# A fused attention and two-mixture kernel: the first unit gets its own stage order, its loads go to two queues, and the order of the first weight loads changes

## The chip, the cores and the metric

The kernel runs on one core of a Trainium2 chip. The metric is the time of one execution in device microseconds (us), and the time of a kernel is the median of three runs. A core has a matrix engine (TensorE, PE in the rows, with its weight loads as PEld), a vector engine (VectorE, DVE), an activation engine (ScalarE, ACT), GpSimd (POOL) and a queue engine (SyncE, SP) that mostly starts loads and stores. ScalarE can start loads too. Each engine works through its own list of instructions in order, and semaphores tie the lists together.

## The reference, cut to what matters

```python
# attention: B, H, S, D = 2, 8, 768, 48
for t in range(S):
    state = alpha[:, :, t, :, None] * state + np.einsum('bhd,bhe->bhde', k[:, :, t], v[:, :, t])
    y[:, :, t] = np.einsum('bhd,bhde->bhe', q[:, :, t], state)
# first mixture: 1536 tokens, 384 features, 4 experts, 1024 hidden
p = domain_probs / (domain_probs.sum(-1, keepdims=True) + 1e-09)
for e in range(E):
    out += p[:, e:e + 1] * (np.maximum(x @ w1[e], 0.0) @ w2[e])
# second mixture: 8 experts, the best two of each token by noisy logits, the same two products
```

## The kernel before, in words

The attention is done in chunks of 128 tokens. Tokens come in seven units of 128 or 256 tokens (`sizes`). A unit is worked through in groups of 128 x 256 values: unit 0 has two groups, here called 0 and 1, unit 1 has the four groups 2 to 5. A group goes through seven stages: `decays` (transpose alpha, running products on VectorE), `keys` (transpose k, scale it on VectorE to K, then on ScalarE to G), `queries` (transpose q, scale to Q), `scores` (G times Q, masked on VectorE to M), `keys_back` (transpose K back, copied by ScalarE to Kn), `states` (Kn times v, added by VectorE to the running state S) and `outputs` (Q times S plus M times v, copied by ScalarE to xn). When all groups of a unit are done, `back` transposes xn into xh and xl, which feed the dense products. `plan()` gives every stage of every group a step number, and `stream()` issues the stages step by step. The first two groups are "near": their stages lie closer together than those of later groups.

While the first attention units are worked through, TensorE also runs `busy(n)`: n filler products of ones by ones whose result nobody reads. `IDLE` says ahead of which stage how many stand.

The first mixture's expert 0 starts as soon as unit 0 is back. Its first phase of 128 tokens is eight dense products f0 to f7 (`hidden`, line 475, straight from the loaded weights `raw`), with the stages of groups 2 to 5 set between them by `drive()`, and then its second products (`product`, lines 494 to 496). Each dense product's result is copied by ScalarE (hh) and VectorE (hl). At each step of `drive()`, `W.step` may prepare one part of the weights: ScalarE casts it to the high part (line 142) and GpSimd subtracts for the low part (line 143). Expert 0's parts 0 to 3 are the four quarters of w2, loaded into spare room of the tile `acc`; parts 4 to 7 are the quarters of w1, loaded into `raw`. They are prepared in the order 0 to 7. The loads of unit 0, of unit 1 and of these eight parts are issued on SP in the order of one loop near the end of the function, which is the only thing that sets their order.

Of the kernel before, what the change touches and what calls it, by code (L numbers as in the profile page):

```python
# [10 lines left out]
F32 = mybir.dt.float32  # L11
# [6 lines left out]
OP = mybir.AluOpType  # L18
AX = mybir.AxisListType

P = 128
# [7 lines left out]
def kernel(  # L29
# [28 lines left out]
    BM = UM // P  # L58
    KD = DM // P
    KF = FF // P  # L60
    HP = H // 2
# [5 lines left out]
    const = ctx.enter_context(tc.tile_pool(name="const", bufs=1))  # L67
# [5 lines left out]
    def ps(tag, bufs=1):  # L73
        return psum.tile([P, 512], F32, tag=tag, name=tag, bufs=bufs)
# [111 lines left out]
    def busy(n):  # L186

        t = ps("g", 4)
        for _ in range(n):
            nc.tensor.matmul(t.rearrange("x (c i) -> x c i", c=4), ones_b, ones_b[:, None, :].to_broadcast([P, 4, P]),  # L190
                             start=True, stop=True)

    busy(14)
    ident = const.tile([P, P], F32, name="ident")
    make_identity(nc, ident)
    tri = const.tile([P, P], F32, name="tri")
# [16 lines left out]
    apool = att.enter_context(tc.tile_pool(name="apool", bufs=1))  # L213
# [4 lines left out]
    for nm, n in (("a", 2), ("k", 1), ("q", 1)):  # L218
        for i in range(n):
            t = apool.tile([P, BM, H, 64], F32, name=f"x_{nm}{i}", tag=f"x_{nm}{i}")  # L220
# [8 lines left out]
    V = {}  # L229

    def inputs(nm, u):
        if nm == "a":
            return X[nm, u % 2]
        return X[nm, 0] if u else early[:, "kq".index(nm)]

    def load_unit(u, names, p0=0, p1=HP):

        if u >= NU:
            return
        b, h0 = divmod(starts[u], S)  # L240
        hs = slice(2 * p0, 2 * p1)
        for nm in names:
            if nm == "v":
                V[u] = apool.tile([P, BM, H, D], F32, tag="v", name="v", bufs=2)
            for c in range(sizes[u] // P):
                frm = src[nm][b, hs, h0 + c * P:h0 + (c + 1) * P, :].rearrange("h p d -> p h d")
                if nm == "v":
                    nc.sync.dma_start(V[u][:, c, hs], frm)
                    continue
                nc.sync.dma_start(inputs(nm, u)[:, c, hs, :D], frm)  # L250


    prob = const.tile([P, NB, E1], F32, name="prob")
    nc.scalar.dma_start(prob, moe_domain_probs.rearrange("(b p) e -> p b e", p=P))
    noise = const.tile([P, NB, E2], F32, name="noise")
    nc.scalar.dma_start(noise, moe2_noise.rearrange("(b p) e -> p b e", p=P))
    wgn = const.tile([P, KD, 2 * E2], F32, name="wgn")
    nc.scalar.dma_start(wgn[:, :, :E2], moe2_w_gate.rearrange("(c p) e -> p c e", p=P))
    nc.scalar.dma_start(wgn[:, :, E2:], moe2_w_noise.rearrange("(c p) e -> p c e", p=P))

    W = Weights()

# [2 lines left out]
    for i in range(2):  # L265
        t = apool.tile([P, UM], F32, name=f"suffix{i}")
# [11 lines left out]
    def attention(u):  # L278

        b, h0 = divmod(starts[u], S)  # L280
# [10 lines left out]
            return slice(i * P, (i + 1) * P)  # L291

        def transposed(nm, g):
            t = ps("tr", 2)
            for i, (p, c) in enumerate(groups[g]):
                nc.tensor.transpose(t[:, at(i)], inputs(nm, u)[:, c, 2 * p:2 * p + 2, :].rearrange("x h d -> x (h d)"), ident)  # L296
            return t[:, :UM]
# [43 lines left out]

        def scores(g):
            A, K, Q, G, rc = st[g]
            t = [ps("sc0"), ps("sc1")]
            for i in range(BM):
                for j in range(2):
                    rows = slice(64 * j, 64 * j + D)
                    nc.tensor.matmul(t[j][:, at(i)], G[rows, at(i)], Q[rows, at(i)], start=True, stop=True)  # L348
            for j in range(2):
                M = apool.tile([P, BM, P], F32, tag=f"M{j}", name="M")  # L350
                nc.vector.tensor_mul(M, t[j][:, :UM].rearrange("x (c i) -> x c i", c=BM),
                                     tri[:, None, :].to_broadcast([P, BM, P]))
                st[g, j] = M
# [23 lines left out]

        def outputs(g):
            A, K, Q, G, rc = st[g]
            t = ps("sc1")  # L380
            for i, (p, c) in enumerate(groups[g]):
                inter = not (first and c == 0)
                if inter:
                    nc.tensor.matmul(t[:, i * 2 * D:(i + 1) * 2 * D], Q[:, at(i)], St[p][:, slot(c), :],  # L384
                                     start=True, stop=False)
                for j in range(2):
                    o = i * 2 * D + j * D
                    nc.tensor.matmul(t[:, o:o + D], st[g, j][:, i, :], V[u][:, c, 2 * p + j, :], start=not inter,  # L388
                                     stop=not inter or j == 1)
            if g == 0:  # L390
                st["xn"] = apool.tile([P, BM, DM], F32, tag="xn", name="xn")
            xn = st["xn"]
            p = groups[g][0][0]
            n = 2 * D * BM // UB
            nc.scalar.activation(xn[:, :UB, 2 * p * D:2 * p * D + n],
                                 t[:, :UB * n].rearrange("x (c d) -> x c d", c=UB), AF.Copy)
# [34 lines left out]
    suffixes = itertools.cycle(suffix)  # L431

    rows_at = {}
    NEAR = 2

    IDLE = {(2, 0): 5, (1, 0): 5, (2, 1): 2, (1, 1): 4, (2, 2): 4, (1, 2): 2, (0, 0): 1, (0, 1): 1, (0, 2): 1}

    def plan():
        at = {}
        base = 0  # L440
        k = 0
        for u in range(NU):
            n, UB, stages, back = attention(u)
            for g in range(n):
                near = k < NEAR
                for order, (stage, off) in enumerate(zip(stages, (5, 4, 1, 3, 3, 2, 0) if near else (7, 6, 1, 5, 3, 2, 0))):
                    at.setdefault(base + off, []).append((order, k, stage, g))
                end = base + (5 if near else 7)
                base += 2 if near else 3
                k += 1  # L450
            for c in range(UB):
                at.setdefault(end + 1 + c, []).append((-1, k, back, c))
            rows_at[u] = end + 1 + UB
        return at

    steps = plan()

    def stream():
        for i in range(max(steps) + 1):
            for order, k, f, g in sorted(steps.get(i, ()), key=lambda z: z[:2]):  # L460
                busy(IDLE.get((order, k), 0))
                f(g)
            yield

# [65 lines left out]
    def drive(main, side=None, n_main=1, n_side=1, bg=None, finish=True):  # L530


        due = 0.0
        pace = n_main / n_side if n_side else float("inf")
        wait = pace
        for _ in main:
            if bg is not None:
                bg()
            due += 1
            while side is not None and due >= wait:  # L540
                due -= wait
                try:
                    said = next(side)
                    wait = pace if said is None else said
                except StopIteration:
                    side = None
        if side is not None and finish:
            for _ in side:
                pass


    psm = const.tile([P, NB], F32, name="psm")
    nc.vector.reduce_sum(psm, prob, axis=AX.X)
    nc.vector.tensor_scalar(psm, psm, 1e-9, None, op0=OP.add)
    nc.vector.reciprocal(psm, psm)
    nc.vector.tensor_mul(prob, prob, psm[:, :, None].to_broadcast([P, NB, E1]))

    for i in range(2):
        load_unit(0, "akq", i * HP // 2, (i + 1) * HP // 2)
    load_unit(0, "v")  # L560
    for what in ("a", "k", "q", 4, 0, 5, "v", 1, 6, 2, 7, 3):
        if type(what) is int:
            W.fetch(what)
        else:
            load_unit(1, what)
    W.n_raw = 2 * NG
# [3 lines left out]
    def until(i):  # L570
        nonlocal now
        while now < i:
            now += 1
            next(rows_now, None)
            yield

    for _ in until(rows_at[0]):
        if now >= 15 and W.n_prep < 4:
            W.prep()

    def n_moe(n):
        return KF + n // P * (KF // 2)
# [4 lines left out]
    for i, (t0, n) in enumerate(phases):  # L587
        for _ in until(rows_at[unit_of(t0 + n)]):
            pass
        nxt = rows_at[unit_of(sum(phases[i + 1]))] if i + 1 < len(phases) else now  # L590
        drive(moe1(0, t0, n), until(nxt), n_moe(n), (nxt - now) * 1.1, W.step)
    att.close()

    hst = ExitStack()
    hidden_in.append((hst.enter_context(tc.tile_pool(name="hpool", bufs=1, side="right")), 4 * P))


    NS = E2 * SB
    BL = 3
# [554 lines left out]
```

## Time and profile before

| | |
|---|---|
| median of three runs | 764.56 us (764.32 to 765.46) |
| the profiled execution | 764.46 us, its span 762.7 us |
| TensorE busy | 98% of the span |
| VectorE, ScalarE, GpSimd busy | 46%, 32%, 21% |

The span is the time from the first to the last instruction; 1.8 us of the execution lie around it. Busy shares are averages over the whole span: TensorE is the engine to look at, and only the first 40 us have other engines in its way.

### The profile page before, as it was taken

The page shows a single profiled execution, that of the slowest core. Times are in us where ns is not written, and L with a number is a line of the kernel's source. Part 1 is how long each engine was busy: PE and PEld are TensorE (multiplying, and loading weights), DVE is VectorE, ACT ScalarE, POOL GpSimd, SP SyncE. Part 2 cuts the span into 40 slices and gives each one's busy share as a digit, 9 for nine tenths or more (in the row PEclk, how much of TensorE's full clock was granted, in tenths as well). Part 3 has the DMA queues.
Part 4 walks back from the last instruction along what each step waited for, and adds up shares of the span by engine and source line. Part 5 has one row for each costly group of instructions (what it writes and reads, how often), then busy time and mean ns, then how long its engine had stood idle before and what let it go on. Part 6 is the DMA issues. An engine that isn't in the chain of part 4 may idle for free.

```text
span 762.7 us, 11958 instructions
## 1 busy us (share of the span) xinstructions
PE 750.6 (98%) x4658; PEld 707.6 (93%) x4658; DVE 351.4 (46%) x864; ACT 246.0 (32%) x481; POOL 160.6 (21%) x174
## 2 busy tenths in 40 slices
PE   9999999999999999999999999999999999999996
PEld 5899999999998989899899999989999999999996
DVE  5877566663222131222212346366745554654641
ACT  2643322232311031211223323333525444444430
POOL 2520000001510023100124100011352424424331
PEclk9999999999999999999999999999999999999999
DMA  9836212100620012100023300011763554654710
GB/s 187 221 75 125 52 32 43 22 1 8 209 75 1 0 42 83 43 0 1 22 63 103 94 21 12 32 42 29 220 206 122 186 161 148 212 161 136 228 63 32
DMA packets 97998, 66.97 MB, mean 88 GB/s; under 512 B 57577, under 2 KB 94500, under 8 KB 97936
## 3 DMA queue, kind: packets, MB, share of 16 engines
q1 hardware_dynamic: 89008, 51.92, 24.6%
q0 software_dynamic: 5024, 14.13, 5.8%
q8 instruction: 39, 0.64, 0.4%
q10 hardware_dynamic: 3904, 0.10, 0.4%
q14 instruction: 23, 0.19, 0.1%
HBM read 56.69 MB, written 9.82 MB: 87 GB/s over the span
## 4 chain that ended last, share of the span: by engine, by line
PE 93%; DVE 5%; ACT 1%; issue 0%; POOL 0%; POOLq 0%; DVEq 0%
PE g L480 13%; PE g L479 13%; PE g L481 13%; PE g L494 10%; PE g L496 10%; PE g L495 10%; PE g L994 3%; PE g L996 3%; PE g L995 3%; PE sc L388 2%; PE tr L296 2%; PE sc L348 2%; PE tr L927 1%; PE sc L362 1%; PE sc L384 1%; PE g L190 1%
## 5 line engine op out<-in xcount | busy, mean ns | idle before, releaser
L485 ACT ACTIVATE hh<-g 128x384 fp32r<-128x384 f32 (+8 forms) x200 | 96.9, 485 | 281.2 <-PE g L481 261.6
L486 DVE SCALAR_TENSOR_TENSOR hl<-g,hh 128x384 fp32r<-128x384 f32 (+8 forms) x200 | 109.5, 550 | 159.5 <-ACT hh L485 154.1
L494 PE MATMUL g<-w2h,hl 128*128 128x384 f32 x464 | 161.7, 348 | 0.0
L496 PE MATMUL g<-w2h,hh 128*128 128x384 f32 x464 | 156.5, 337 | 0.0
L495 PE MATMUL g<-w2l,hh 128*128 128x384 f32 x464 | 156.4, 337 | 0.0
L479 PE MATMUL g<-xh,w1l 128*128 128x512 f32 (+2 forms) x360 | 127.0, 353 | 0.0
L480 PE MATMUL g<-xl,w1h 128*128 128x512 f32 (+2 forms) x360 | 124.4, 346 | 0.0
L481 PE MATMUL g<-xh,w1h 128*128 128x512 f32 (+2 forms) x360 | 124.3, 345 | 0.0
L143 POOL TENSOR_TENSOR w1l<-raw,w1h 128x768 fp32r<-128x768 f32 x16 | 29.3, 1841 | 280.2 <-ACT w1h L142 280.2
L494 PEld LDWEIGHTS g<-w2h,hl 128*128 128x128 f32 x464 | 87.3, 188 | 0.5
L495 PEld LDWEIGHTS g<-w2l,hh 128*128 128x128 f32 x464 | 87.4, 188 | 0.3
L496 PEld LDWEIGHTS g<-w2h,hh 128*128 128x128 f32 x464 | 87.2, 188 | 0.0
L523 DVE SCALAR_TENSOR_TENSOR acc<-g,prob,acc 128x384 f32<-128x384 f32 x36 | 22.2, 618 | 119.7 <-PE g L496 119.7
L480 PEld LDWEIGHTS g<-xl,w1h 128*128 128x128 f32 x360 | 67.8, 188 | 6.3 <-DVE xl L413 0.3
L481 PEld LDWEIGHTS g<-xh,w1h 128*128 128x128 f32 x360 | 67.7, 188 | 6.3
L479 PEld LDWEIGHTS g<-xh,w1l 128*128 128x128 f32 x360 | 67.8, 188 | 6.0
L479 PE MATMUL g<-xth,w1l 128*128 128x256 f32 (+6 forms) x216 | 73.2, 339 | 0.0
L480 PE MATMUL g<-xtl,w1h 128*128 128x256 f32 (+6 forms) x216 | 71.4, 331 | 0.1
L481 PE MATMUL g<-xth,w1h 128*128 128x256 f32 (+6 forms) x216 | 71.3, 330 | 0.0
L142 ACT ACTIVATE w2h<-raw 128x768 fp32r<-128x768 f32 x44 | 36.4, 843 | 35.3 <-issue 23.0
L945 POOL DMA_INDIRECT out_dram<-yo,si_c x26 | 26.1, 1004 | 87.1 <-DVE yo L944 80.9
L994 PE MATMUL g<-hh,w2l 128*128 128x432 f32 (+4 forms) x120 | 43.3, 361 | 0.0
(193 smaller groups left out, 1056.1 us busy)
## 6 DMA issues: line engine op xcount, KB each, us to landing
raw<-in_moe_w_dram SPq DMA_DIRECT2D x92, 384.0 KB, 4.3
v<-in_v_dram SPq DMA_DIRECT2D x12, 192.0 KB, 2.9
out_dram<-zero SPq DMA_DIRECT2D x1, 2304.0 KB
x2d<-acc SPq DMA_DIRECT2D x12, 192.0 KB, 4.5
x_a<-in_alpha_dram SPq DMA_DIRECT2D x20, 96.0 KB, 2.1
x_k<-in_k_dram SPq DMA_DIRECT2D x18, 96.0 KB, 2.6
x_q<-in_q_dram SPq DMA_DIRECT2D x18, 96.0 KB, 2.7
acc<-in_moe_w_dram SPq DMA_DIRECT2D x4, 384.0 KB, 7.1
```

Source lines behind the costliest of these rows:

```text
L142: nc.scalar.activation(hi, r, AF.Copy)
L143: (nc.gpsimd if e < E1 or own else nc.vector).tensor_sub(lo, r, hi.bitcast(F32))
L479: nc.tensor.matmul(t[:, :n], wl, hx[:, kd, t0:t0 + n], start=(kd == 0), stop=False)
L480: nc.tensor.matmul(t[:, :n], wh, lx[:, kd, t0:t0 + n], start=False, stop=False)
L481: nc.tensor.matmul(t[:, :n], wh, hx[:, kd, t0:t0 + n], start=False, stop=(kd == KD - 1))
L485: nc.scalar.activation(hh[:, :n], t[:, :n], AF.Relu)
L486: nc.vector.scalar_tensor_tensor(hl[:, :n], t[:, :n], 0.0, hh.bitcast(F32)[:, :n], op0=OP.max, op1=OP.subtract)
L494: nc.tensor.matmul(t[:m, :DM], hl[:, o:o + m], wh, start=(f == 0), stop=False)
L495: nc.tensor.matmul(t[:m, :DM], hh[:, o:o + m], wl, start=False, stop=False)
L496: nc.tensor.matmul(t[:m, :DM], hh[:, o:o + m], wh, start=False, stop=(f == KF - 1))
L945: nc.gpsimd.indirect_dma_start(out=parts_of_out[s], out_offset=bass.IndirectOffsetOnAxis(ap=SLOT[e * SB + s][2][:n, e * SB + s:e * SB + s ...
L994: nc.tensor.matmul(t[:, :n], wl, hh[:, :n], start=(f == 0), stop=False)
```

## The change

Unit 0's groups get step numbers of their own (`NEAR`), in which the transposed-back keys and the states come last, behind `back`. Their k and q loads are issued by ScalarE instead of SP. 21 of the 39 fillers go. The loads of the noise and of the gate weights move from the front to behind the last phase of expert 0, the sum of the probabilities moves behind expert 0's first eight dense products, and the probabilities are loaded by SP. Some tiles of unit 0 are taken from the four banks of the dense products ("g") and no longer from "tr", "sc0" and "sc1". And the loop that loads unit 1 and the eight weight parts has another order.

```diff
-    busy(14)
+    busy(9)
...
-    def load_unit(u, names, p0=0, p1=HP):
+    def load_unit(u, names, p0=0, p1=HP, queue=nc.sync):
...
+    for i in range(2):
+        load_unit(0, "a", i * HP // 2, (i + 1) * HP // 2)
+        load_unit(0, "kq", i * HP // 2, (i + 1) * HP // 2, nc.scalar)
+    load_unit(0, "v")
 
     prob = const.tile([P, NB, E1], F32, name="prob")
-    nc.scalar.dma_start(prob, moe_domain_probs.rearrange("(b p) e -> p b e", p=P))
     noise = const.tile([P, NB, E2], F32, name="noise")
-    nc.scalar.dma_start(noise, moe2_noise.rearrange("(b p) e -> p b e", p=P))
...
-            t = ps("tr", 2)
+            t = ps("g", 4) if u == 0 and (nm, g) in (("q", 0), ("a", 1)) else ps("tr", 2)
...
-            t = [ps("sc0"), ps("sc1")]
+            t = [ps("g", 4), ps("g", 4)] if u == 0 and g else [ps("sc0"), ps("sc1")]
...
-    NEAR = 2
-
-    IDLE = {(2, 0): 5, (1, 0): 5, (2, 1): 2, (1, 1): 4, (2, 2): 4, (1, 2): 2, (0, 0): 1, (0, 1): 1, (0, 2): 1}
+    NEAR = ({"decays": 0, "keys": 0, "queries": 0, "scores": 2, "outputs": 4, "keys_back": 7, "states": 8},
+            {"decays": 0, "keys": 1, "queries": 1, "scores": 3, "outputs": 5, "keys_back": 8, "states": 9})
+    FAR = {"decays": 0, "keys": 1, "queries": 2, "keys_back": 3, "scores": 5, "states": 6, "outputs": 7}
...
+    IDLE = {("scores", 0): 2, ("scores", 1): 5, ("back", 1): 2}
...
-    psm = const.tile([P, NB], F32, name="psm")
-    nc.vector.reduce_sum(psm, prob, axis=AX.X)
...
-    for what in ("a", "k", "q", 4, 0, 5, "v", 1, 6, 2, 7, 3):
+    for what in ("a", "k", 4, "q", 5, "p", "v", 6, 7, 0, 1, 2, 3):
...
-        drive(moe1(0, t0, n), until(nxt), n_moe(n), (nxt - now) * 1.1, W.step)
+        drive(moe1(0, t0, n, None if i else probabilities), until(nxt), n_moe(n), (nxt - now) * 1.1, W.step)
...
+    nc.sync.dma_start(noise, moe2_noise.rearrange("(b p) e -> p b e", p=P))
+    nc.sync.dma_start(wgn[:, :, :E2], moe2_w_gate.rearrange("(c p) e -> p c e", p=P))
```

On ScalarE, from the back-transposed unit 0 on, the list of before reads as follows (x32 is the 128 x 384 piece of `acc`; `w2h<-acc` is the cast of a w2 part, `hh<-g` the copy behind a dense product, `G<-K` and `Kn<-tr` belong to the attention's groups):

```order
L411 ACTIVATE acc<-g 128x384 [waits PE_49]
L412 ACTIVATE xh<-g 128x3x128
L321 ACTIVATE G<-K,rc 128x128 [waits DVE_49]
L321 ACTIVATE G<-K,rc 128x128
L485 ACTIVATE hh<-g 128x128 [waits PE_49]
L142 ACTIVATE w2h<-acc 128x768 [waits DMAHW2_49]
L485 ACTIVATE hh<-g 128x128 [waits PE_49]
L142 ACTIVATE w2h<-acc 128x768 [waits DMAHW6_49]
L339 ACTIVATE Kn<-tr 128x256 [waits PE_49,Activation_49]
L485 ACTIVATE hh<-g 128x128 [waits PE_49]
L142 ACTIVATE w2h<-acc 128x768 [waits DMAHW0_49]
```

And in the changed kernel, from the same place on:

```order
L412 ACTIVATE acc<-g 128x384 [waits PE_49]
L413 ACTIVATE xh<-g 128x3x128
L498 ACTIVATE hh<-g 128x128 [waits PE_49]
L142 ACTIVATE w2h<-acc 128x768 [waits DMAHW4_49]
L340 ACTIVATE Kn<-tr 128x256 [waits PE_49]
L498 ACTIVATE hh<-g 128x128 [waits PE_49]
L142 ACTIVATE w2h<-acc 128x768 [waits DMAHW5_49]
L322 ACTIVATE G<-K,rc 128x128 [waits DVE_49,Activation_49]
L322 ACTIVATE G<-K,rc 128x128
L340 ACTIVATE Kn<-tr 128x256 [waits PE_49]
L498 ACTIVATE hh<-g 128x128 [waits PE_49]
L142 ACTIVATE w2h<-acc 128x768 [waits DMAHW6_49]
```

The casts of the w2 parts stand at the same dense products as before, but the Kn of unit 0's two groups, which stood far ahead of the first cast, now stand behind the first and the second one.

On SP, behind the loads of unit 0 and the first four of unit 1, the list of before reads (a `raw` load is a w1 part, an `acc` load from `in_moe_w_dram` a w2 part):

```order
L250 DMA x_q_114<-in_q_dram 128x8x48 [waits DMAHW0_49]
L119 DMA raw<-in_moe_w_dram 128x3x256 [waits DMAHW1_49]
L124 DMA acc<-in_moe_w_dram 128x2x384 [waits DMAHW2_49]
L119 DMA raw<-in_moe_w_dram 128x3x256 [waits DMAHW3_49]
L248 DMA v<-in_v_dram 128x8x48 [waits DMAHW4_49]
L248 DMA v<-in_v_dram 128x8x48 [waits DMAHW5_49]
L124 DMA acc<-in_moe_w_dram 128x2x384 [waits DMAHW6_49]
L119 DMA raw<-in_moe_w_dram 128x3x256 [waits DMAHW7_49]
L124 DMA acc<-in_moe_w_dram 128x2x384 [waits DMAHW0_49]
```

And now:

```order
L250 DMA x_q_109<-in_q_dram 128x8x48 [waits DMAHW5_49]
L119 DMA raw<-in_moe_w_dram 128x3x256 [waits DMAHW6_49]
L569 DMA prob<-in_moe_domain_probs_dram 128x12x4 [waits DMAHW7_49]
L248 DMA v<-in_v_dram 128x8x48 [waits DMAHW0_49]
L248 DMA v<-in_v_dram 128x8x48 [waits DMAHW1_49]
L119 DMA raw<-in_moe_w_dram 128x3x256 [waits DMAHW2_49]
L119 DMA raw<-in_moe_w_dram 128x3x256 [waits DMAHW3_49]
L124 DMA acc<-in_moe_w_dram 128x2x384 [waits DMAHW4_49]
L124 DMA acc<-in_moe_w_dram 128x2x384 [waits DMAHW5_49]
```

The first w2 part was the second weight load on the queue; it is now the fifth, behind all four w1 parts and all of unit 1.

On TensorE, behind the first two dense products (the first `g<-acc,raw` here ends f1), the changed kernel has this (`sc<-v,Kn` is `states`, `sc<-Q,G` is `scores`, `tr<-ident,K` is `keys_back`):

```order
L488 MATMUL g<-acc,raw 128x128 x3
L363 MATMUL sc_346<-v,Kn 128x96 [waits Activation_49]
L363 MATMUL sc_346<-v,Kn 128x96
L297 MATMUL tr<-ident,x_k_107 128x128 [waits PE_49]
L297 MATMUL tr<-ident,x_k_107 128x128
L338 MATMUL tr<-ident,K 128x128 [waits DVE_49]
L338 MATMUL tr<-ident,K 128x128
L488 MATMUL g<-acc,raw 128x128 [waits DMAHW6_49]
L488 MATMUL g<-acc,raw 128x128 x2
L363 MATMUL sc_379<-v,Kn 128x96 [waits DVE_49,Activation_49]
L363 MATMUL sc_379<-v,Kn 128x96
L349 MATMUL sc_387<-Q,G 128x128 [waits DVE_49,PE_49]
```

In the kernel before, the `states` of groups 0 and 1 stood ahead of the first dense product, with fillers around them; no filler stands in this stretch now. From the `states` of group 5 on, TensorE's list is the same in both kernels to the end.

## Rows read from the trace of the kernel before

**Rows 1.** Busy time by stretch: busy us per engine (instructions), then clock, DMA share, GB/s.

```profile
0.00:10.00 10.00, 8.53 (x39) 4.11 (x39) 4.75 (x18) 1.98 (x3) 4.07 (x20) 1.00 0.95 124
10.00:20.00 10.00, 9.66 (x70) 6.91 (x68) 6.99 (x25) 3.26 (x10) 0.00 (x0) 1.00 1.05 251
20.00:30.00 10.00, 9.25 (x78) 7.99 (x79) 7.76 (x27) 6.46 (x17) 6.22 (x4) 1.00 0.88 249
40.00:200.00 160.00, 159.43 (x1229) 152.86 (x1228) 93.92 (x277) 49.44 (x127) 12.57 (x7) 1.00 0.24 52
```

**Rows 2.** Timeline, 0 to 28.5 us: first fillers, first scan, first dense product, three casts.

```profile
1.13 4.90 PE L190 MATMUL g<-ones_b 128*128 128x512 bf16 x14 [1.13 <-DVE ones_b L185]
...
4.51 1.01 PEld L190 LDWEIGHTS <-ones_b 128*128 128x128 bf16 x5 [0.28 <-issue]
...
6.36 0.73 DVE L312 TENSOR_TENSOR_SCAN suffix<-tr,tri 128x127 f32<-128x127 f32 x2 [1.00 <-PE tr L296]
...
20.23 0.94 PE L475 MATMUL g<-acc,raw 128*128 128x128 f32 x6 [0.34 <-ACT acc L411]
...
22.61 0.83 ACT L142 ACTIVATE w2h<-acc 128x768 fp32r<-128x768 f32 x1
...
26.23 0.84 ACT L142 ACTIVATE w2h<-acc 128x768 fp32r<-128x768 f32 x1 [0.71 <-DMA acc<-in_moe_w_dram]
```

**Rows 3.** Timeline of TensorE, 27 to 41 us, between the last waits and the merge.

```profile
27.53 0.72 PE L348 MATMUL sc<-Q,G 48*128 48x128 f32 x8
...
29.00 0.69 PE L362 MATMUL sc<-v,Kn 128*128 128x96 f32 x4 [0.39 <-DVE M L351]
...
30.62 0.36 PE L384 MATMUL sc<-S,Q 128*128 128x96 f32 x2
...
31.90 0.40 PE L296 MATMUL tr<-ident,x_k 128*128 128x128 f32 x2
...
32.14 0.83 PE L475 MATMUL g<-acc,raw 128*128 128x128 f32 x6
...
32.90 0.71 PE L348 MATMUL sc<-Q,G 48*128 48x128 f32 x8
...
40.04 0.58 PE L362 MATMUL sc<-v,Kn 128*128 128x96 f32 x4
```

**Rows 4.** DMA queues in the first 8 us: packets, MB, share of 16 engines.

```profile
q10 hardware_dynamic: 3904, 0.10, 34.4%
```

**Rows 5.** Instruction groups by shape, 5.6 to 40.1 us, ScalarE, then VectorE.

```profile
L321 ACT ACTIVATE G<-K,rc 128x128 f32<-128x128 f32 x14 | 4.9, 394 | 8.5 <-DVE K L319 8.4
L142 ACT ACTIVATE w2h<-acc 128x768 fp32r<-128x768 f32 x4 | 3.4, 840 | 0.7 <-DMA acc<-in_moe_w_dram 0.7
L339 ACT ACTIVATE Kn<-tr 128x256 f32<-128x256 f32 x6 | 2.3, 376 | 1.6 <-PE tr L337 1.5
...
L312 DVE TENSOR_TENSOR_SCAN suffix<-tr,tri 128x127 f32<-128x127 f32 x14 | 5.1, 407 | 1.8 <-PE tr L296 1.5
L314 DVE TENSOR_TENSOR_SCAN A<-tr,tri 128x128 f32<-128x128 f32 x14 | 5.0, 398 | 0.0
L351 DVE TENSOR_TENSOR M<-sc,tri 128x256 f32<-128x256 f32 x12 | 4.5, 416 | 0.1
L319 DVE TENSOR_TENSOR K<-tr,suffix 128x256 f32<-128x256 f32 x7 | 2.9, 410 | 0.0
L372 DVE COPY S<-sc 48x48 f32<-48x48 f32 x8 | 1.6, 205 | 2.3 <-PE sc L362 1.2 <-PE tr L296 1.1
```

**Rows 6.** Timeline of VectorE, 5 us: the last of the four probability instructions.

```profile
5.14 0.21 DVE L556 TENSOR_TENSOR prob<-prob,psm 128x48 f32<-128x48 f32 x1
```

**Rows 7.** The gate weights' readers: first and last start in us.

```profile
L652 PEld LDWEIGHTS sc<-wgn,x2T x72: 187/192/192, 419.9 to 520.3; 128*128 128x128 f32 x72
```

**Rows 8.** Busy time at the end of the span, columns as in Rows 1.

```profile
756.00:758.00 2.00, 0.70 (x5) 0.39 (x3) 0.62 (x1) 0.00 (x0) 0.36 (x1) 1.00 0.03 6
759.00:760.00 1.00, 0.00 (x0) 0.00 (x0) 0.00 (x0) 0.00 (x0) 0.00 (x0) 0.50 0.37 129
```

More of the change, by code (lines that the diff above doesn't have):

```diff
@@ L247, in load_unit @@
                 if nm == "v":
-                    nc.sync.dma_start(V[u][:, c, hs], frm)
+                    queue.dma_start(V[u][:, c, hs], frm)
                     continue
-                nc.sync.dma_start(inputs(nm, u)[:, c, hs, :D], frm)
+                queue.dma_start(inputs(nm, u)[:, c, hs, :D], frm)
+    for i in range(2):
+        load_unit(0, "a", i * HP // 2, (i + 1) * HP // 2)
+        load_unit(0, "kq", i * HP // 2, (i + 1) * HP // 2, nc.scalar)
+    load_unit(0, "v")
     prob = const.tile([P, NB, E1], F32, name="prob")
-    nc.scalar.dma_start(prob, moe_domain_probs.rearrange("(b p) e -> p b e", p=P))
     noise = const.tile([P, NB, E2], F32, name="noise")
-    nc.scalar.dma_start(noise, moe2_noise.rearrange("(b p) e -> p b e", p=P))
     wgn = const.tile([P, KD, 2 * E2], F32, name="wgn")
-    nc.scalar.dma_start(wgn[:, :, :E2], moe2_w_gate.rearrange("(c p) e -> p c e", p=P))
-    nc.scalar.dma_start(wgn[:, :, E2:], moe2_w_noise.rearrange("(c p) e -> p c e", p=P))
     W = Weights()
@@ L349, in scores @@
             for j in range(2):
-                M = apool.tile([P, BM, P], F32, tag=f"M{j}", name="M")
+                M = apool.tile([P, BM, P], F32, tag=f"M{j}", name="M", bufs=2)
                 nc.vector.tensor_mul(M, t[j][:, :UM].rearrange("x (c i) -> x c i", c=BM),
@@ L379, in outputs @@
             A, K, Q, G, rc = st[g]
-            t = ps("sc1")
+            t = ps("g", 4) if u == 0 and g else ps("sc1")
             for i, (p, c) in enumerate(groups[g]):
@@ L433 @@
     rows_at = {}
-    NEAR = 2
-    IDLE = {(2, 0): 5, (1, 0): 5, (2, 1): 2, (1, 1): 4, (2, 2): 4, (1, 2): 2, (0, 0): 1, (0, 1): 1, (0, 2): 1}
+    NEAR = ({"decays": 0, "keys": 0, "queries": 0, "scores": 2, "outputs": 4, "keys_back": 7, "states": 8},
+            {"decays": 0, "keys": 1, "queries": 1, "scores": 3, "outputs": 5, "keys_back": 8, "states": 9})
+    FAR = {"decays": 0, "keys": 1, "queries": 2, "keys_back": 3, "scores": 5, "states": 6, "outputs": 7}
+    ORDER = ("outputs", "states", "keys", "scores", "keys_back", "queries", "decays")
+    IDLE = {("scores", 0): 2, ("scores", 1): 5, ("back", 1): 2}
     def plan():
         at = {}
-        base = 0
+        base = 4
         k = 0
@@ L444, in plan @@
             for g in range(n):
[L445 to L449, printed above, removed]
+                offs = NEAR[k] if k < len(NEAR) else {nm: base + off for nm, off in FAR.items()}
+                if k == len(NEAR):
+                    offs["keys_back"] = 9
+                for order, (stage, nm) in enumerate(zip(stages, ORDER)):
+                    if k == 0 and nm in ("keys", "queries"):
+                        order += 10
+                    elif k == 1 and nm == "decays":
+                        order += 20
+                    elif k == 0 and nm == "decays":
+                        order = 0
+                    at.setdefault(offs[nm], []).append((order, k, stage, g, nm))
+                end = offs["outputs"]
+                if k >= len(NEAR):
+                    base += 3
                 k += 1
             for c in range(UB):
-                at.setdefault(end + 1 + c, []).append((-1, k, back, c))
+                at.setdefault(end + 1 + c, []).append((-1, k - 1, back, c, "back"))
             rows_at[u] = end + 1 + UB
@@ L459, in stream @@
         for i in range(max(steps) + 1):
-            for order, k, f, g in sorted(steps.get(i, ()), key=lambda z: z[:2]):
-                busy(IDLE.get((order, k), 0))
+            for order, k, f, g, nm in sorted(steps.get(i, ()), key=lambda z: z[:2]):
+                busy(IDLE.get((nm, k), 0))
                 f(g)
@@ L549, in drive @@
                 pass
-    psm = const.tile([P, NB], F32, name="psm")
-    nc.vector.reduce_sum(psm, prob, axis=AX.X)
[L554 to L560, printed above, removed]
-    for what in ("a", "k", "q", 4, 0, 5, "v", 1, 6, 2, 7, 3):
+    for what in ("a", "k", 4, "q", 5, "p", "v", 6, 7, 0, 1, 2, 3):
         if type(what) is int:
             W.fetch(what)
+        elif what == "p":
+            nc.sync.dma_start(prob, moe_domain_probs.rearrange("(b p) e -> p b e", p=P))
         else:
@@ L577, with probabilities @@
     for _ in until(rows_at[0]):
-        if now >= 15 and W.n_prep < 4:
-            W.prep()
+        pass
+    psm = const.tile([P, NB], F32, name="psm")
+    def probabilities():
+        nc.vector.reduce_sum(psm, prob, axis=AX.X)
+        nc.vector.tensor_scalar(psm, psm, 1e-9, None, op0=OP.add)
+        nc.vector.reciprocal(psm, psm)
+        nc.vector.tensor_mul(prob, prob, psm[:, :, None].to_broadcast([P, NB, E1]))
     def n_moe(n):
@@ L595 @@
     hidden_in.append((hst.enter_context(tc.tile_pool(name="hpool", bufs=1, side="right")), 4 * P))
+    nc.sync.dma_start(noise, moe2_noise.rearrange("(b p) e -> p b e", p=P))
+    nc.sync.dma_start(wgn[:, :, :E2], moe2_w_gate.rearrange("(c p) e -> p c e", p=P))
+    nc.sync.dma_start(wgn[:, :, E2:], moe2_w_noise.rearrange("(c p) e -> p c e", p=P))
     NS = E2 * SB
```

## The prediction

> **What bounds the kernel now.** I read the stretches of the span first. From 40 to 200 us TensorE is busy for 159.43 of 160 us, and the page gives it 98% of the whole span; only the first three stretches of 10 us have gaps, 8.53, 9.66 and 9.25 [rows 1]. Then I compared the lists of both kernels. From the `states` of group 5 on, at 40.04 us [rows 3], TensorE has the same list in both, so whatever the change is worth is the shift of that one instruction, called the merge here. Behind it TensorE waits for nothing for long, so the shift should reach the end as it is. Last I read the timeline up to the merge. What the reader is to see there: the first dense product starts at 20.23, the first cast of a w2 part at 22.61 without a wait, the third only at 26.23, after 0.71 us of waiting for its load [rows 2]. From the `scores` of group 3 at 27.53 to the merge TensorE then runs almost without a gap [rows 3]. And the DMA engines move 251 and 249 GB/s in the second and third 10 us, shares of 1.05 and 0.88 [rows 1]: loads are as close to a bound there as TensorE is.
>
> **What it removes.** 21 fillers. The last five of the opening ones took 1.01 us, 0.20 each [rows 2], so at most 21 x 0.20 = 4.2 us of TensorE's time is freed. Most of those fillers stood where TensorE would have waited, so this is a ceiling and no term of the sum. The tiny loads at the front: 3904 packets on ScalarE's queue took 34.4% of 8 us, 2.75 us of the DMA engines [rows 4]. The 1536 packets of the probabilities stay in the early stream, so 2368/3904 of it, 1.7 us, goes.
>
> **What costs nothing.** The noise and gate weights are first read at 419.9 us [rows 7]; their loads now stand behind the last phase of expert 0, with three more experts of the first mixture to come before anything reads them, and would cost only if SP came to them later than that. The four probability instructions, at most 0.21 each, 0.84 us [rows 6], now run on VectorE while TensorE has the first two pairs of second products, six matmuls, ahead of it; without that cover they would cost 0.84. Groups 0 and 1 in "g" banks wait for nothing else, since the dense products are not there yet.
>
> **When the first dense product is ready.** Five fillers fewer start the first scan 1.0 us earlier, at 5.3 instead of 6.36 [rows 2], if alpha and k have landed. Ahead of group 2's G, VectorE then has the scans of three decays (2 x 0.407 + 2 x 0.398 = 1.6 each), three K, two Q of about the same length and four M: 4.8 + 1.2 + 0.8 + 1.7 = 8.5 us [rows 5], so 13.8. Two G of 0.39 [rows 5], a copy of unit 0 and the dense product of 0.76 (32.14 to 32.90) [rows 3] lead to a first cast that ScalarE could start at 16 to 17, six us earlier than now.
>
> **What it waits for there.** The first w2 part is now the fifth weight load. Ahead of it stand unit 0 with 768 KB, unit 1 with 1536, the probabilities with 24 and four w1 parts with 1536; with its own 384 that is 4248 KB, 4.35 MB. Before, 1.24 + 2.51 MB had been moved by 20 us and the rest would take 0.60/0.249 = 2.4 more [rows 1]: 22.4, less the 1.7 from above, 20.7 us. The same sum for the third w2 part of the kernel before (4704 KB with everything ahead) gives 24.3, where ScalarE in fact waited until 26.23 [rows 2], 1.9 later. So the first part lands between 20.7 and 22.6; I take the middle, 21.6. ScalarE stands in front of that cast for about 5 us. Queued behind it are the Kn of group 0, the next hh and the G of group 3. TensorE can still do f1 and then needs that Kn for the `states` of group 0, so it stops too, and VectorE with it. Nothing fills this hole: the fillers are gone from there.
>
> **The way from there to the merge.** Each step now needs the one before on another engine. From the start of the cast: cast 0.84, Kn 0.38, `states` 0.69, four copies into S 0.82, K 0.41, two G 0.79, the second Kn 0.38, `states` 0.69, four copies 0.82, `scores` of group 2 0.71 (these share the bank sc0, so they follow the copies), `keys_back` 0.24 (as the pair at 31.90 to 32.14), Kn 0.38, `states` 0.69, `keys_back` 0.24, alpha's transpose 0.24, f3 0.76, `outputs` 1.28 (30.62 to 31.90), k's transpose 0.24, f4 0.76 [rows 3, 5]. Sum 11.4, with nothing for the handing over. The second and third w2 parts, about 1.6 us apart (0.39 MB at 0.249 per us), are there when their casts come up. So the `scores` of group 3 start at 21.6 + 11.4 = 33.0, against 27.53. From there to the merge the kernel before took 40.04 - 27.53 = 12.51 [rows 3]. One dense product of 0.76 is already done, but the dense product and the second products that stood between `scores` and `states` in groups 4 and 5 now stand ahead of them, so that the wait of 0.39 for M [rows 3] comes twice more: 12.51 - 0.76 + 0.78 = 12.5. The merge comes at 45.5, 5.5 us later than before.
>
> **The clock.** Nine fillers from 1.13 to 4.51 took 0.38 each, the next ones 0.20 [rows 2]: half rate, then full, after back-to-back work. At the end the granted clock is still 1.00 in 756 to 758, where the last matmuls end after 0.70 us, and 0.50 in 759 to 760 [rows 8]: 1.2 GHz, after TensorE had been idle. The hole forecast here, from about 17 to 22.8, is longer than that idle time, so the clock probably falls. Between nothing (it holds) and all TensorE steps of the way above once more (0.69 three times, 0.71, four times 0.24, two 0.76, 1.28, together 6.5) I take the two `states` right behind the hole at double length, 1.4 us, since then the engine works again. The Trainium skill ("TensorE: Matmul & The Clock Gate", part 1, what's actually happening) says that half rate is the default and activity releases it; by that the fall is sure and paid once per hole, and the sum would stay as it is.
>
> **The sum.** 5.5 + 1.4 = 6.9 us on the profiled execution's own 764.46 (span 762.7 and 1.8 around it), 771.4; the median of the runs lies 0.1 above that execution, so **771.5 us**.
>
> **The rivals.**
> 1. *The stretch behind the hole refills.* If the steps overlap better than my chain, TensorE's own work decides: up to the `scores` of group 3 it has three `states` (2.07), one `scores` (0.71), seven pairs of transposes (1.68), three dense products (2.28) and `outputs` (1.28), 8.0 us in place of the chain behind Kn, and no new waits. Then the merge is at 21.6 + 1.2 + 8.0 + 11.75 = 42.6, +2.5, 767.1; with the early landing of 20.7, 766.2. For it: VectorE's load of about 7 us in 10 [rows 1]. Against: bank sc0 and the order of ScalarE, which tie the steps.
> 2. *The clock stays at half through the broken stretch.* 5.5 + 6.5 = 12 us, 776.6. For it: the steps there are short and far between. Against: no row here shows such gaps, since fillers stood in them. The Trainium skill ("TensorE: Matmul & The Clock Gate", a second HAM failure mode) tells of a kernel in which short idle times between groups of matmuls made the clock swing; no run here shows it yet.
> 3. *Faster: the w2 part is there when ScalarE comes.* The hole vanishes and the freed filler time counts, at most 4.2 us, 760.4. It turns at a landing of about 16 (21.6 less the 5.5 lost). That needs 4.35 MB in the 14 us from 2 to 16, 310 GB/s, where the rows show 251 with the engines full [rows 1]. Two queues would have to add up; the Trainium skill ("DMA: Bandwidth & Descriptors", issuing engines are not separate DMA queues) says that they share the same engines.
> 4. *No difference:* an early landing, a clock that holds and a tight stretch together use up the loss, 763.0 to 766.1.
>
> **How the numbers follow.** A measurement of this kernel tells about 0.2%, 1.5 us, from no change. Chances: the forecast, 767.5 to 774.5, 0.60; rival 1 above the 0.2%, 766.1 to 767.5, 0.14; rival 2 or a still later landing, above 774.5, 0.10; no difference 0.10; faster 0.06. My low sum is 20.7 + 11.4 + 11.75 = 43.85, +3.8, 768.3; the high one 22.6 and 6.5, +13, 777.5. The range reaches down to the edge of "no difference" and up into rival 2: 766.0 to 776.5. Slower 0.84, same 0.10, faster 0.06.
>
> **What would show it.** In the profile after: the first dense product at 15 to 16; the first cast of a w2 part idle for some 5 us, released by its load, and starting between 20.7 and 22.6; TensorE idle from about 17 until that cast, its wait named Kn; a granted clock of 0.50 somewhere between 19 and 27; `states` of group 5 near 47. Wrong it would be if the first cast starts below 18, or if TensorE is busy for more than 9 of the 10 us from 20 to 30 although the cast waits.

## The result and the profile after

The changed kernel takes 773.16 us (median of four runs, 772.32 to 774.05) where the kernel before takes 764.96: a ratio of 1.0108 (95% interval 1.0090 to 1.0125), by which it is 8.3 us slower. The execution that was profiled is the slowest of the four, 774.05 with a span of 772.3, which is 9.6 more than the span before.

The busy time by stretch comes first, with the columns of [rows 1].

```profile
0.00:10.00 10.00, 7.35 (x36) 3.62 (x36) 5.31 (x19) 2.67 (x5) 4.07 (x20) 1.00 0.94 176
10.00:20.00 10.00, 6.46 (x53) 5.29 (x51) 5.40 (x17) 2.38 (x7) 0.00 (x0) 1.00 1.06 262
20.00:30.00 10.00, 6.14 (x29) 5.41 (x30) 3.10 (x13) 3.98 (x9) 5.43 (x3) 0.56 0.70 191
30.00:40.00 10.00, 9.52 (x65) 8.64 (x63) 6.27 (x22) 4.16 (x11) 3.63 (x2) 0.75 0.28 54
60.00:200.00 140.00, 139.96 (x1093) 133.96 (x1092) 84.56 (x251) 42.60 (x113) 4.01 (x3) 1.00 0.20 39
```

TensorE's busy time, the first figure behind the length, falls from 9.66 and 9.25 [rows 1] to 6.46 and 6.14, and its clock (third from the right) to 0.56 and 0.75. From 60 us on it is busy throughout, as before (159.43 of 160 us from 40 us on [rows 1]): the loss is made by 40 us and carried to the end. The same view in steps of 2 us, for TensorE alone (busy us, clock, DMA share, GB/s):

```profile
18.00:20.00 2.00, 0.00 (x0) 1.00 1.02 354
20.00:22.00 2.00, 0.00 (x0) 0.82 1.06 385
22.00:24.00 2.00, 1.69 (x8) 0.50 1.13 312
...
32.00:34.00 2.00, 2.00 (x12) 0.50 0.43 82
34.00:36.00 2.00, 2.00 (x17) 0.76 0.00 0
```

There is the hole: TensorE does nothing from 18 to 22 us while the DMA engines are full. By the clock column TensorE is at half rate, 1.2 GHz, for some 13.7 us, from about 21.3 to 35.0. The timeline (start, duration, engine, line, and in brackets the wait and who ended it), with rows that answer to [rows 2, 3]:

```profile
5.09 0.73 DVE L313 TENSOR_TENSOR_SCAN suffix<-tr,tri 128x127 f32<-128x127 f32 x2 [2.87 <-PE tr L297]
...
15.24 0.94 PE L488 MATMUL g<-acc,raw 128*128 128x128 f32 x6 [1.04 <-ACT acc L412]
...
21.14 0.84 ACT L142 ACTIVATE w2h<-acc 128x768 fp32r<-128x768 f32 x1 [4.65 <-DMA acc<-in_moe_w_dram]
22.31 1.17 PE L363 MATMUL sc<-v,Kn 128*128 128x96 f32 x4 [4.66 <-ACT Kn L340]
...
28.33 1.23 PE L349 MATMUL sc<-Q,G 48*128 48x128 f32 x8 [1.11 <-DVE S L373]
...
32.52 1.49 PE L488 MATMUL g<-acc,raw 128*128 128x128 f32 x6
33.80 0.58 PE L385 MATMUL sc<-S,Q 128*128 128x96 f32 x2
...
35.62 0.40 PE L297 MATMUL tr<-ident,x_k 128*128 128x128 f32 x2
...
36.62 0.71 PE L349 MATMUL sc<-Q,G 48*128 48x128 f32 x8
...
38.08 0.69 PE L363 MATMUL sc<-v,Kn 128*128 128x96 f32 x4 [0.38 <-DVE M L352]
...
49.34 0.69 PE L363 MATMUL sc<-v,Kn 128*128 128x96 f32 x4 [0.30 <-DVE M L352]
```

The first dense product is 5.0 us earlier than before, the first cast of a w2 part 1.5 earlier (21.14 against 22.61 [rows 2]), yet the `scores` of group 3 come at 36.62 against 27.53 and the merge at 49.34 against 40.04 [rows 3]: 9.3 of the 9.6. The cast waits 4.65 for its load, and the `states` of group 0 wait 4.66 for the Kn behind that cast. Afterwards the same kinds of instructions last longer than at the full clock: `states` 1.17 against 0.69 at 38.08, `scores` 1.23 against 0.71 at 36.62, the dense product 1.49 against the usual 0.83. The list of waits from 5 to 50 us (total, times, longest) shows that VectorE waits behind the same cast, by way of hh:

```profile
DVE hl L499 <- ACT hh L498: 7.0, 4, 3.9
...
ACT w2h L142 <- DMA acc<-in_moe_w_dram: 5.7, 2, 4.7
PE sc L363 <- ACT Kn L340: 5.1, 2, 4.7
```

### The profile page after: what moved, and what is told of

It is laid out like the page before. It is cut to its first block, busy times and chain, and to the rows that moved or that the text cites. A ratio compares the mean times of both kernels' runs of the same rounds, so it can differ in the third digit from the quotient of the medians.

```text
span 772.3 us, 11913 instructions
## 1 busy us (share of the span) xinstructions
PE 751.0 (97%) x4637; PEld 709.5 (92%) x4637; DVE 352.7 (46%) x864; ACT 247.0 (32%) x481; POOL 161.5 (21%) x174
## 4 chain that ended last, share of the span: by engine, by line
PE 90%; DVE 5%; SPq 1%; ACT 1%; DMA 1%; issue 1%; POOL 0%; POOLq 0%; DVEq 0%; ACTq 0%
PE g L493 13%; PE g L492 13%; PE g L494 13%; PE g L507 10%; PE g L509 10%; PE g L508 10%; PE g L1011 3%; PE g L1013 3%; PE g L1012 3%; PE sc L389 2%; PE tr L297 2%; PE sc L349 2%; PE sc L363 2%; PE tr L944 1%; PE sc L385 1%; PE sc L669 1%
```

## The experiments

Ratios are to the kernel before on the same chip, whose median beside the experiments was 764.4 to 765.1. The last column is the ratio less 1, times 765.

| run | median us | ratio (95% interval) | us |
|---|---|---|---|
| the change | 773.16 | 1.0108 (1.0090 to 1.0125) | +8.3 |
| e1: old order of loads | 768.97 | 1.0056 (1.0042 to 1.0069) | +4.3 |
| e2: hole filled | 772.46 | 1.0112 (1.0096 to 1.0127) | +8.6 |
| e3: before, new order of loads | 764.91 | 1.0007 (0.9998 to 1.0017) | +0.5 |
| e4: late casts | 765.51 | 1.0013 (1.0004 to 1.0022) | +1.0 |
| e5: Kn early | 772.63 | 1.0100 (1.0083 to 1.0118) | +7.7 |
| e6: late casts, filled | 763.52 | 0.9983 (0.9974 to 0.9992) | -1.3 |
| e7: before, loads alone | 765.07 | 0.9999 (0.9990 to 1.0008) | -0.1 |
| e8: late casts, Kn early | 764.73 | 0.9996 (0.9987 to 1.0005) | -0.3 |
| e9: the change, new places | 771.27 | 1.0089 (1.0074 to 1.0105) | +6.8 |
| e10: before, new places | 761.95 | 0.9963 (0.9950 to 0.9977) | -2.8 |
| e11: late casts, old places | 768.58 | 1.0042 (1.0029 to 1.0056) | +3.2 |
| e12: late casts, Kn early, filled | 762.69 | 0.9969 (0.9957 to 0.9981) | -2.4 |

### The order of loads (e1, e3)

```diff
-    for what in ("a", "k", 4, "q", 5, "p", "v", 6, 7, 0, 1, 2, 3):
+    for what in ("a", "k", "q", 4, 0, 5, "p", "v", 1, 6, 2, 7, 3):
```

> The changed kernel with the load order of before put back (k, q, w1 part 4, w2 part 0, 5, probabilities, v, 1, 6, 2, 7, 3); all else as changed. Theory A (the loss is the first w2 cast standing at the head of ScalarE's list while its load is fifth in the queue, and the half clock that follows): the cast starts near 16.5 without a wait, no 0.50 clock, merge at 38 to 41 us, time 761 to 765. Rival B (the new stage order is itself slower, since states and keys_back now form a chain behind the dense products with no fillers): the hole goes but the chain stays, merge at 43 or later, time 768 or more.

The other way round, in the kernel before:

```diff
-    for what in ("a", "k", "q", 4, 0, 5, "v", 1, 6, 2, 7, 3):
+    for what in ("a", "k", 4, "q", 5, "v", 6, 7, 0, 1, 2, 3):
```

> The kernel before with nothing changed but the order of the loads (all w1 parts, then all w2 parts). Theory A: its first cast comes only at 22.6, the first w2 part lands at 22 to 23, so the four casts wait about 0 to 2 us in all and Kn of the first groups is long done: 764.5 to 767. Rival D (the load order alone costs what was measured): 771 or more.

e1 gives back about half of the loss, so the 761 to 765 of its first theory are missed; 768.97 and a merge at 44.36 are what Rival B gave. The first cast no longer waits, but its timeline shows that the wait has moved to the second and third cast rather than gone, and the clock still falls, to 0.50 from 24 to 30 us:

```profile
16.46 0.84 ACT L142 ACTIVATE w2h<-acc 128x768 fp32r<-128x768 f32 x1
19.75 0.84 ACT L142 ACTIVATE w2h<-acc 128x768 fp32r<-128x768 f32 x1 [1.71 <-DMA acc<-in_moe_w_dram]
23.25 0.84 ACT L142 ACTIVATE w2h<-acc 128x768 fp32r<-128x768 f32 x1 [1.65 <-DMA acc<-in_moe_w_dram]
...
44.36 0.69 PE L363 MATMUL sc<-v,Kn 128*128 128x96 f32 x4 [0.30 <-DVE M L352]
```

In e3 the new order costs nothing that can be measured, as its Theory A has it, though the first cast waits there too, 1.49 us at 23.90. In these runs the order hurts only where the casts are early.

### The hole and the clock (e2)

```diff
-    IDLE = {("scores", 0): 2, ("scores", 1): 5, ("back", 1): 2}
+    IDLE = {("scores", 0): 2, ("scores", 1): 5, ("back", 1): 2, ("states", 0): 21}
```

> The changed kernel with 21 fillers (about 4.5 us at full clock) ahead of the states of group 0, where TensorE stood idle from 17.6 to 22.3; loads and order as changed. Theory A with the clock as a term of its own: the cast still waits 4.6 us, the clock stays at 1.00, and the way from the cast to the scores of group 3 falls from 15.5 to 12 us: time 769 to 770.5. Rival C (the half clock costs little, since VectorE and ScalarE set the pace of that stretch): 772.5 to 773.5.

The cast still waits 4.9 us, TensorE runs fillers meanwhile, and its clock holds through the hole. It falls later, behind two stretches that were not filled (first TensorE by stretch, columns as above, then the first cast and the `scores` of group 3):

```profile
20.00:22.00 2.00, 2.00 (x10) 1.00 1.06 383
...
24.00:26.00 2.00, 0.54 (x5) 1.00 0.55 116
26.00:28.00 2.00, 0.89 (x10) 1.00 0.18 32
28.00:30.00 2.00, 1.69 (x14) 0.77 1.11 224
30.00:32.00 2.00, 2.00 (x11) 0.50 0.99 187
```

```profile
21.38 0.84 ACT L142 ACTIVATE w2h<-acc 128x768 fp32r<-128x768 f32 x1 [4.94 <-DMA acc<-in_moe_w_dram]
...
34.68 0.72 PE L349 MATMUL sc<-Q,G 48*128 48x128 f32 x8
```

Half rate lasts some 3.4 us in place of 13.7, yet the median is that of the change within the spread: Theory A's 769 to 770.5 are missed, and 772.46 lies at the lower end of Rival C's 772.5 to 773.5. The two profiled executions lie 2.4 us apart, but one is the fastest of its kernel (771.61) and the other the slowest of its own (774.05). So filling the hole alone brings nothing that the medians can tell, and by this pair what the clock costs in the changed kernel stays open between nothing and about 2.4 us.

### The casts out of the way (e4)

```diff
-            self.rest = 0
+            self.rest = 4
```

The first cast then stands behind the fifth dense product in ScalarE's list.

> The changed kernel with the first cast put off by four steps (it then stands behind the fifth dense product and not the first); loads and order as changed. Theory A: nothing of the attention stands behind a cast that waits for its load, no hole, no 0.50 clock; the casts and GpSimd's low parts (four of 1.8 us) then end later, and the second products may wait some us for them: 761 to 767. Rival B (the stage order itself): 768 or more.

The first cast starts at 32.03 without a wait, the `scores` of group 3 at 31.37, 5.25 earlier than in the change. The clock still fell, against its Theory A (the rows stand with e6 below). The time came down by 7.3 us, more than that shift explains. The rest was elsewhere: TensorE's list is the same in both, but its dense products over 512 columns were shorter. The groups of TensorE's instructions from 200 to 400 us (busy us, mean ns of one), first in the changed kernel, then here:

```profile
L492 PE MATMUL g<-xh,w1l 128*128 128x512 f32 x144 | 56.8, 395 | 0.0
```

```profile
L492 PE MATMUL g<-xh,w1l 128*128 128x512 f32 x144 | 56.1, 389 | 0.0
```

Where tiles lie in the weight pool follows from the order in which they are first asked for. With late casts the hidden tiles hh and hl of f0 to f4 come ahead of the w2 parts, and the rest of them ahead of the w1 parts: the w2 parts lie higher too, and the w1 parts by 10368 bytes (the pairs of f5 to f7, 432 values of 4 bytes in each tile). e9 to e11 below test the layout.

### Kn ahead of the casts (e5, e8)

```diff
-    NEAR = ({"decays": 0, "keys": 0, "queries": 0, "scores": 2, "outputs": 4, "keys_back": 7, "states": 8},
-            {"decays": 0, "keys": 1, "queries": 1, "scores": 3, "outputs": 5, "keys_back": 8, "states": 9})
+    NEAR = ({"decays": 0, "keys": 0, "queries": 0, "scores": 2, "outputs": 4, "keys_back": 5, "states": 8},
+            {"decays": 0, "keys": 1, "queries": 1, "scores": 3, "outputs": 5, "keys_back": 6, "states": 9})
```

> The changed kernel with the turning back of K of groups 0 and 1 issued earlier (keys_back at steps 5 and 6 in place of 7 and 8), so that their two Kn stand ahead of the first cast on ScalarE; loads, casts and fillers as changed. Theory A (what is queued behind the waiting cast is the loss, not the wait itself): the first cast still waits for its load until about 21, but states of groups 0 and 1 and the scores of group 2 are done in the hole; only the G of group 3, behind the second cast (25.0 in the changed kernel), still waits. Scores of group 3 at 27 to 31 instead of 36.6, median 764 to 769. Rival B (the waiting casts hold everything back whatever stands ahead of them, or the clock takes the gain): scores of group 3 later than 33, median over 770.

Theory A missed: the `scores` of group 3 start at 34.01 and the median is 772.63, as Rival B has it. The `states` of group 0 do come ahead of the hole, but those of group 1 now stop there, for 4.99 us. Rows of VectorE and TensorE in its timeline:

```profile
22.45 0.29 DVE L499 SCALAR_TENSOR_TENSOR hl<-g,hh 128x128 fp32r<-128x128 f32 x1 [3.84 <-ACT hh L498]
22.65 0.89 DVE L373 COPY S<-sc 48x48 f32<-48x48 f32 x4
...
23.68 1.15 PE L363 MATMUL sc<-v,Kn 128*128 128x96 f32 x4 [4.99 <-DVE S L373]
```

Not only Kn stands behind the cast on ScalarE, the next hh does too. VectorE's hl waits for that hh, the copies into S stand behind hl, and the next `states` need their bank back from the copies. The waiting cast thus holds up VectorE and TensorE behind ScalarE in two ways, by Kn and by hh. Freeing Kn alone gains 0.6 us by the ratios, with intervals that overlap.

With the casts late, the same edit:

> The changed kernel with the casts begun behind the fifth dense product and the turning back of K of groups 0 and 1 at steps 5 and 6. Theory A (with the casts out of the way, what remains is the wait for Kn of group 1, 1.59 us, and then for the copies into S, 1.11): the first wait goes, the second stays; scores of group 3 at 29.5 to 31, merge 1 to 2 us earlier, median 763.5 to 765. Rival B (the half clock is what remains and comes anyway): median 765 to 766, the same as with late casts alone.

The `scores` of group 3 come at 30.23, 1.1 earlier than in e4; by the ratio it is 1.3 us, and the two intervals overlap. The 764.73 lies where Theory A put it, but in place of the wait for Kn there is one of 1.04 for S, the next one for S has grown to 1.84, and the clock still falls.

### The clock again, with the casts gone (e6, e12)

```diff
-    IDLE = {("scores", 0): 2, ("scores", 1): 5, ("back", 1): 2}
+    IDLE = {("scores", 0): 2, ("scores", 1): 5, ("back", 1): 2, ("states", 1): 8, ("scores", 2): 6}
```

In e6 this edit stands on top of e4. In e12 it stands on top of e8, with 5 and 9 fillers.

> The changed kernel with the casts begun behind the fifth dense product (as in the run of late casts), and 8 fillers ahead of the states of group 1 and 6 ahead of the scores of group 2, where TensorE waited 1.59 and 1.11 us there and the clock then fell to half for 6.8 us. Theory A (the half clock is what is left of the loss): the clock stays at 1.00 from 10 us on, the dense product of the fourth kind takes 0.8 instead of 1.49, the scores of group 3 start 1 to 3 us earlier than 31.4, median 762 to 764.5. Rival B (the chain of handovers is what is left, TensorE's rate does not matter there): the clock holds but the median stays at 765 to 766. Rival C (fillers delay the states): 766 or more.

> The changed kernel with the casts begun behind the fifth dense product, the two K turned back at steps 5 and 6, and 5 fillers ahead of the states of group 1 and 9 ahead of the scores of group 2. Theory A (with the casts gone, Kn early and the clock held, what remains is the chain from the copies into S to the scores of group 2): clock 1.00 from 10 us on, scores of group 3 at 27.5 to 29, median 762 to 763.5. Rival B (the fillers are in the way, or the clock falls elsewhere): 763.5 to 765.

Both came in as Theory A has it. TensorE by stretch in e4, then in e6:

```profile
20.00:22.00 2.00, 0.46 (x4) 1.00 1.04 376
22.00:24.00 2.00, 0.89 (x9) 0.65 1.13 328
24.00:26.00 2.00, 1.89 (x11) 0.50 0.97 192
```

```profile
20.00:22.00 2.00, 2.00 (x12) 1.00 1.08 388
22.00:24.00 2.00, 2.00 (x16) 1.00 1.11 323
24.00:26.00 2.00, 1.69 (x16) 1.00 0.52 108
```

The fillers go into waits of 1.59 and 1.11 us, the clock stays at 1.00, and the `scores` of group 3 start 2.4 us earlier, at 28.96. By the ratios the fillers are worth 2.3 us (e4 to e6) and 2.1 (e8 to e12). Without them the clock was at half for some 6.8 us in e4.

### The loads alone (e7)

The kernel before, with k and q of unit 0 on ScalarE's queue, noise and gate weights late, and the probabilities loaded by SP and summed behind the first dense products. Stage order, fillers and the order of the weight parts are those of before.

```diff
+        load_unit(0, "kq", i * HP // 2, (i + 1) * HP // 2, nc.scalar)
...
-    for what in ("a", "k", "q", 4, 0, 5, "v", 1, 6, 2, 7, 3):
+    for what in ("a", "k", "q", 4, 0, 5, "p", "v", 1, 6, 2, 7, 3):
```

> The kernel before with the load part alone: unit 0's k and q on ScalarE's queue, noise and gate weights loaded behind expert 0's phases, probabilities loaded behind two w2 parts and summed behind the first dense products; stage order, fillers, order of the weight parts and the point of the first cast as before. Theory A (the loads bring little because the first scan and the first dense product wait for other work): the first dense product at 19 to 20.3, the wait of 0.71 us before the third cast goes, median within 1.5 us of before, 763 to 766. Rival B (the tiny loads and the one queue held the start up): first dense product before 18.5 and median under 763.

No change in time: 765.07 on both sides. The casts no longer wait for their loads, as expected; the first dense product is 1.0 later (21.26), not earlier. Its 14 opening fillers took 5.93 us, against 4.90 in the profile of before [rows 2], and the shift of 1.0 stays up to the merge (41.05 against 40.04 [rows 3]). These fillers read no load, and the same 14 took 4.60 in e3 and 5.21 in e10, so their length differs between executions; that the loads had a part in the 5.93 is not shown. One profile alone can be 1 us off here, and the verdict rests on the medians.

### The places in SBUF (e9, e10, e11)

The tiles are only asked for earlier; no instruction is added, removed or moved. e9 (the change) and e10 (the kernel before) get the layout of e4, by the lines shown; e11 is e4 with the layout of before, for which it asks for the hidden tiles of f0, the w2 parts, those of f1 to f4 and then the w1 parts.

```diff
+    def place(tags, n, f):
+        for tag in tags:
+            for _ in range(n):
+                wpool.tile([P, f], F32 if tag == "raw" else F32R, tag=tag, name=tag, bufs=n)
...
+    place(("raw",), 4, part)
+    hidden_places(0, 5)
+    place(("w2h", "w2l"), NG, part)
+    hidden_places(5, 8)
```

> The changed kernel with the tiles of the weight pool laid out in SBUF as they came to lie in the runs with late casts (the hidden tiles hh and hl of the first five f ahead of the w2 parts, the rest ahead of the w1 parts, so that the w1 parts start 10368 bytes higher); no instruction is added, removed or moved. Theory A (the late casts gained in two ways, and one of them is where the w1 parts lie: their dense products of 512 columns took 389 ns each against 394 to 395, so that 2.5 us came off behind 150 us): those products take 389 ns here too, the stretch up to the merge is as in the changed kernel, median 769.5 to 771.5, 2 to 3.5 us under 773.2. Rival B (the faster dense products come from the order of casts, not from the places): 394 to 395 ns, median 772 to 774.

> The kernel before with the tiles of the weight pool laid out as in the runs with late casts; no instruction is added, removed or moved. Theory A (places): dense products of 512 columns at 389 ns, median 761.5 to 763, ratio near 0.997, better than both kernels and at least as good as the late casts with fillers (763.5). Rival B (order of casts): 394 to 395 ns, median as before, 764 to 765.5.

> The changed kernel with the casts begun behind the fifth dense product, the tiles of the weight pool laid out as in the kernel before. Theory A (places are worth 2.5 us of what late casts gave): dense products of 512 columns at 394 to 395 ns, median 767.5 to 769, so that of the 8.7 us lost the casts at the head of ScalarE's list carry 5 to 6 and the handing over with the half clock 3 to 4. Rival B (places do nothing): median 765 to 766, as with late casts alone.

All three medians fell where Theory A put them. The same group in e10, then in e11:

```profile
L494 PE MATMUL g<-xh,w1l 128*128 128x512 f32 x144 | 56.1, 389 | 0.0
```

```profile
L508 PE MATMUL g<-xh,w1l 128*128 128x512 f32 x144 | 56.8, 395 | 0.0
```

The layout alone is worth 2.8 us on the kernel before (e10), 2.2 between e11 and e4, and 1.5 on the change (e9, where the intervals overlap). Over the whole span of e10 the groups agree: the three groups of w1 products over 512 columns save 0.7 to 0.8 us each, the three of the first mixture over 384 columns 0.3 to 0.4 each. Its w2 products, whose tiles moved as well, keep their 348, 337 and 337 ns. **e10 beats both kernels, by 0.37% and 1.4%,** without the change. e12 has the same layout and is not clearly different (the intervals overlap), so the change's stage order, repaired, gains nothing on the old one that these runs can tell.

## Why the prediction was right, point by point

- **The merge decides.** It moved by 9.3, the span by 9.6. Right.
- **First scan and first dense product.** 5.09 and 15.24 for 5.3 and 15 to 16. Right; e1, e2, e4 and e9, with the same stage order, have their first dense product at 15.19 to 15.31.
- **The landing.** The cast began at 21.14, forecast 21.6, between 20.7 and 22.6, after 4.65 of idle time where about 5 was forecast. Right: the sum over the bytes ahead in the stream was good to half a microsecond here. Three more runs with this order of loads and early casts gave 21.38 (e2), 21.41 (e5) and 22.20 (e9), all within the bounds; that the middle was so close is partly luck.
- **The hole.** TensorE stopped for Kn, 4.66 us. Right, but the reason is wider than the prediction's: the hh behind the cast stops VectorE as well (e5).
- **From the cast to the `scores` of group 3.** Forecast 11.4 and 1.4 for the clock; it took 36.62 - 21.14 = 15.5. The clock is the mis-sized term. The steps at half rate make most of the excess of 4.1 over 11.4: three `states` 0.48 each, `scores` 0.51, f3 0.66, `outputs` (33.80 to 35.62) 0.54, together 3.2 where 1.4 was taken. In e2, with the clock up for most of the way, it took 34.68 - 21.38 = 13.3, of which two steps at half rate are 1.1. So the chain without the clock was nearly right, its handing over is worth at most 0.8, and the clock was taken too small, because half rate did not end with the first work behind the hole. How long it lasts differs: in e9, with the same instructions, the clock was back by 28 us and fell once more (rows at the end), and the same way, from the cast at 22.20 to the `scores` at 36.02, took 13.8.
- **From there to the merge.** 12.7 for 12.5. Right. Landing (0.5 early), way (2.7 long) and this (0.2 long) make up the 2.4 by which the merge came later than the forecast 46.9.
- **The clock and the Trainium skill.** The prediction took the fall as paid once per hole and short, and put the lasting half rate into rival 2, within a chance of 0.10. The half rate lasted as rival 2 says, to 35 us, but the price stayed below its 6.5, since the steps took 1.4 to 1.8 times and not twice as long. The Trainium skill ("TensorE: Matmul & The Clock Gate", a second HAM failure mode) tells of short idle times between groups of matmuls that make the clock swing. The traces agree: in e4 the clock fell behind waits of 1.59 and 1.11, and in e9 it fell twice. One reading of the prediction is not borne out by its rows: it took the opening fillers' 0.38 and 0.20 us for half and full rate, while the granted clock stands at 1.00 there [rows 1].
- **Costs nothing.** The gate weights and noise held back nobody. The probabilities' four instructions took 1.28 us (0.19, 0.65, 0.23, 0.21), not 0.84, since the second is a longer one than the row read for all four. The merge waits 0.30 for an M that starts right behind them, so at most 0.3 was not covered.
- **Rivals.** Rival 3 (the load is there in time) would need a landing of 16: it was 21. e1 shows what such a landing gives with its early first cast: the next two casts wait instead. Rival 1 and rival 4 fall with the 15.5.

By the ratios the loss divides as follows, if the parts add up, which no single run shows. Taking the casts from the head of ScalarE's list, with the places held (the change to e11), brings 5.1 of 8.3; the old load order alone (e1), still with early casts, 4.0. Of the 3.2 left, the clock is worth 2.1 to 2.3, as priced with the new places (e4 to e6, e8 to e12). About 1 remains; that it lies in the handing over of the broken stretch is argued and not shown. Read by itself, e4 would have put 7.3 us on the casts: 2.2 of that was where the tiles lay.

## What to carry to other kernels

A cast, or any instruction that waits for a load, holds everything behind it on its engine, and through that the engines that wait for it: when work in front becomes faster, look at what the in-order list reaches earlier and whether its load is there. When fillers are taken out, the gaps that remain must be read for the clock one by one, short ones included. And when an edit changes the order in which tiles are first asked for, compare the length of untouched instructions far behind it, before the gain is put down to the edit.

## What the runs showed that was not expected

**The clock falls without a hole of the length seen in the change, and the same instructions do not always give it the same course.** In e4 TensorE was busy for 0.46 and 0.89 of two stretches of 2 us and then ran at half rate for some 6.8 us, although from 24 to 30 us it was busy for 1.89 or more of every 2. e9 has the change's instructions, only elsewhere in SBUF; there half rate ended and came back (rows below). Nor does every such wait bring the clock down: in e3 TensorE waited 1.45 us ahead of the `states` at 29.99, between stretches of full work, and the clock stayed at 1.00.

```profile
24.00:26.00 2.00, 2.00 (x11) 0.50 0.60 128
26.00:28.00 2.00, 1.35 (x8) 0.74 0.02 3
28.00:30.00 2.00, 1.09 (x12) 1.00 0.50 100
30.00:32.00 2.00, 1.69 (x9) 0.62 1.03 199
```

**A dense product's length depends on where its tiles lie.** 389 against 394 to 395 ns over 512 columns at a clock of 1.00, 335 against 338 over 384 columns for two of the three lines, and no gain over 256 columns (283 against 282, 282 against 281); all of these read w1. Which tile matters (the w1 parts, 10368 bytes higher, or the hidden tiles beside them) and by what mechanism was not tried and stays open.
